# A grouped-query decode block on one core: SyncE keeps the first six loads, GpSimd issues the other 68

## The chip, the core and the metric

The kernel runs on one core of a Trainium2 chip. A core has a matrix engine (TensorE, PE), three engines for elementwise work (VectorE or DVE, ScalarE or ACT, GpSimd or POOL) and an engine for synchronisation and transfers (SyncE, SP). Each runs its own list of instructions in order, and they wait for each other on semaphores. Data comes from the device's memory through 16 DMA engines; SP, ACT and POOL can each issue a transfer, and the DMA engines then carry it out. The metric is the device time of one execution in microseconds (us).

## The reference

Two sequences (B = 2), one token each, are taken through an attention block with a cached history and a gated multilayer perceptron. All is float32.

```
xn = layernorm(x)                                  # x: 2 x 1 x 512
q  = xn @ wq                                       # 32 query heads of 128, 8 key/value heads
s  = softmax(q @ k_cache^T * 128**-0.5) @ v_cache  # 4 query heads share a K/V head
s  = s.reshape(2, 1, 4096) @ wo                    # back to 512
g  = silu((relu(xn @ W_gate) * (xn @ W_up)) @ W_down)   # inner width 1792
out = x + s * g
```

The caches are 2 x 8 x 32768 x 128 each: 268 MB of K and as much of V. All of it is read once, and very little is computed with each byte.

## The kernel before

**Tiles.** For each of the 16 pairs of sequence and K/V head (a group) the 32768 cached tokens are cut into four tiles of 8192 tokens. K and V are loaded two tiles at a time, 8 MB to a load: 128 rows (one for each partition of the on-chip memory) of 64 KB. So there are 32 K loads and 32 V loads; `load_kk(j)` (line 427) and `load_vv(j)` (line 446) issue them for pair j.

**Buffers.** There are three buffers of this size. `kbuf[0]` and `kbuf[1]` take the K pairs in turn, and `wide` takes V. Before that, `wide` holds the query weights wq, then the gate and up weights, then the down weights W_down; at the end, `kbuf[0]` takes one V pair and `kbuf[1]` the output weights wo. A load can be issued when the work that read the buffer's last content is over.

**The loop.** Step j (line 908) does four things: VectorE transposes the K pair j in place in eight pieces (line 679) and TensorE forms its scores (`scores`, line 681); TensorE multiplies the V pair j - 2 by its weights (`values`, line 758); VectorE takes the scores out of the accumulators (line 697); and weights for the next V pair are prepared (lines 748 to 756). A group takes two steps. In odd steps a group's scores are complete: the maximum is found (lines 710 to 738), ScalarE takes the exponentials, and the group whose values are complete is finished: sums (line 775), scaling (line 784), then `finish_group` (line 803), which turns the heads and lets GpSimd copy them into place (line 831). Also in odd steps GpSimd forms the next group's query (`take_query`, lines 544 to 548), when the scores that read the old one are over.

**What sets the order.** Nothing is planned at run time. The program is written as one list of operations (class `Program`, line 31). Each names what it reads and writes, and from that come the waits on other engines; on its own engine each operation keeps its place in the list. So a load waits for its buffer, but it also waits for everything that stands before it on the engine that issues it. Around the change the list of step j reads, shortened:

```
scores(s), [t == 2: mlp_down()], scores(s + 1)   # PE
[odd j: take_query]                              # POOL
values(v), values(v + 1)                         # PE
[odd j: maximum, sums, take_o, finish_group]     # DVE, PE, and POOL at line 831
weights for the next V pair
[j == 0: load_d()  else: load_vv(j - 1)]         # SP
[load_kk(j + 2)]                                 # SP
```

Ahead of the loop SP is given wq, K pair 0, gate, up and K pair 1; in step 0 W_down (`load_d`, line 620) and K pair 2; in step 1 V pair 0 and K pair 3; and so on. After the last step `load_wo` (line 458) issues wo in six pieces. SP has nothing else to do. ScalarE issues two loads of x (4 KB each) and the output.

**Names in the profile.** The K buffers appear as k, `wide` as w, the scores as s, the value sums as o, the down projection as d, the query as qcur. The loads issued by SP have line 248, all matmuls line 251.

Of the kernel before, what the change touches and what calls it, by code (L numbers as in the profile page):

```python
# [167 lines left out]
def decode_block_kernel(nc, x, kc, vc, wq, wo, wg, wu, wd, out):  # L168
# [17 lines left out]
    def sbuf(name, *shape, align=32):  # L186
        return nc.alloc_sbuf_tensor(name, list(shape), F32, align_bytes=align)[:]
# [4 lines left out]
    kbuf = [sbuf(f"k{i}", P, 2 * NC * NR * DH, align=ALIGN) for i in range(2)]  # L192
    wide = sbuf("w", P, 2 * NC * NR * DH, align=ALIGN)
# [53 lines left out]
    def load(dst, src, sem, r=(), w=(), engine="SP"):  # L247
        pg.op(engine, lambda e: e.dma_start(dst, src), r, w, dma=sem)  # L248
# [12 lines left out]
    def group(g):  # L261
        return g % B, g // B
# [50 lines left out]
    for kb in range(4):  # L313
        dve(
            lambda e, kb=kb: e.memset(block_of[Q * kb : Q * kb + Q, kb * REP : (kb + 1) * REP], 1.0),
            w=["block_of"],
# [92 lines left out]
                lambda e, k=k: e.transpose(  # L409
                    px[:, k * 32 : (k + 1) * 32], xquad[:, k, :], ident[:32, :32]  # L410
                )
# [12 lines left out]
    def k_keys(b):  # L424
        return [f"k{b}"] + [f"k{b}_{i}_{c}" for i in range(2) for c in range(NC)]

    def load_kk(j):
        b = j % 2
        load(kbuf[b], rows_of(kc, 2 * j), f"k{b}", w=k_keys(b))

    def rows_of(src, t):
        b, hk = group(t // NU)
        lo = (t % NU) // 2 * 2 * TK
        return src[b, hk, lo : lo + 2 * TK, :].rearrange("(p r) d -> p (r d)", p=P)
# [10 lines left out]

    def load_vv(j):
        if 2 * j == NK - 4:
            load(kbuf[0], rows_of(vc, 2 * j), "k0", w=k_keys(0))
        else:
            load(wide, rows_of(vc, 2 * j), "v", w=["wide"])  # L450

    def in_halves(tokens):
        return tokens.rearrange("p (h c r d) -> p h c r d", h=2, c=NC, d=DH)
# [3 lines left out]
    def load_wo():  # L457
        for quad, cuts in enumerate(((0, 32), (0, 16, 24, 28, 31, 32))):
            dst = kbuf[1][:, quad * ROWS * D : (quad + 1) * ROWS * D]
            WO.append(dst.rearrange("p (j d) -> p j d", j=ROWS))  # L460
            n = ROWS * P
            rows = wo[quad * n : (quad + 1) * n, :].rearrange("(p j) d -> p (j d)", j=ROWS)
            for lo, hi in zip(cuts, cuts[1:]):
                name = f"wo{quad}_{lo}"
                for i in range(lo, hi):
                    WOK[quad, i // 2, i % 2] = name
                load(
                    dst[:, lo * D // 2 : hi * D // 2],
                    rows[:, lo * D // 2 : hi * D // 2],
                    name,  # L470
                    w=[*k_keys(1), name] if quad == 0 else [name],
                )

    def project_q():
# [396 lines left out]
    def project_far():  # L871
# [29 lines left out]
        )  # L901

    load_kk(0)
    project_q()
    load_gu()
    load_kk(1)

    for j in range(PAIRS + 2):
        s, v = 2 * j, 2 * (j - 2)
# [40 lines left out]
        if j == 0:  # L950
            load_d()
        elif j < PAIRS - 1:
            load_vv(j - 1)
        if j == PAIRS - 2:
            load_vv(PAIRS - 2)
        if j + 2 < PAIRS:
            load_kk(j + 2)
        if j == PAIRS - 1:
            load_vv(PAIRS - 1)
            load_wo()  # L960
# [68 lines left out]
```

## Time and profile before

| | us |
|---|---|
| median of three runs | 1309.55 (1309.3 to 1309.71) |
| span of the profiled execution | 1308.7 |
| median less span | 0.85 |
| TensorE busy | 854.4 (65%) |
| VectorE busy | 715.9 (55%) |
| ScalarE busy | 51.3 (4%) |
| GpSimd busy | 12.1 (1%) |
| bytes moved by DMA | 564.81 MB, mean 432 GB/s |

A profile records one execution: when each instruction began, how long it took, and what released the engine that had been idle before it. The rows that are quoted from it have these forms. An instruction in order of time gives its start, its length (both in us), engine, line, operation, what it writes and reads, and in brackets how long its engine had been idle and what ended that. Equal instructions that follow each other are one row with their count; its length reaches from the first to the last. "SPq" and "ACTq" are a queue's own issuing of a transfer. A row of the DMA issues gives the line's tensor, the count, the size, and the time from the issue until the data has landed. A row by stretches gives the stretch, its length, the busy time and the count of instructions of PE, of PE's weight loads, of DVE, ACT and POOL, then the granted clock of TensorE, the busy share of the 16 DMA engines and the GB/s. The row "DMA" with 40 digits is the busy share of the DMA engines, in tenths, in 40 equal slices of the span. "q1" is the queue that SP's loads go through, with its packets, megabytes and share.

### The profile page before, as it was taken

What the parts mean: (1) busy time and instruction counts of PE and PEld (TensorE: products, weight loads), DVE (VectorE), ACT (ScalarE), POOL (GpSimd) and SP (SyncE); (2) the same over time, 40 slices, a digit from 0 to 9 for tenths busy, and PEclk for the clock granted to TensorE, in tenths of its full rate; (3) what the DMA queues carried; (4) which work ended last, traced back from release to release, by engine and by line L of the source; (5) the groups of instructions that cost most, each with busy time, mean ns of one, the idle gap of its engine ahead of it and who ended that gap; (6) DMA issues with size and microseconds to landing.
All of it is one profiled execution on the core that took longest, in us unless ns stands there. A gap on an engine that the chain in (4) does not pass through costs nothing.

```text
span 1308.7 us, 11351 instructions
## 1 busy us (share of the span) xinstructions
PE 854.4 (65%) x4824; PEld 214.3 (16%) x4824; DVE 715.9 (55%) x682; ACT 51.3 (4%) x133; POOL 12.1 (1%) x43
## 2 busy tenths in 40 slices
PE   3566675775566577566667756566765767766685
PEld 1111121211112121111111111111111212111122
DVE  2566554565645466664546665455565545656521
ACT  0001000000000000000000000000000000000000
POOL 0000000000000000000000000000000000000000
PEclk9678788987878888887898788789778788878888
DMA  9999999999999999999999999999999999999998
GB/s 417 425 439 429 441 425 439 425 443 429 437 429 441 427 439 427 439 435 435 441 429 439 427 441 427 439 427 439 445 427 439 429 439 429 439 427 439 435 433 362
DMA packets 10710, 564.81 MB, mean 432 GB/s; under 512 B 1226, under 2 KB 1354, under 8 KB 1612
## 3 DMA queue, kind: packets, MB, share of 16 engines
q1 hardware_dynamic: 10656, 564.66, 99.7%
q8 instruction: 7, 0.11, 0.0%
q14 instruction: 3, 0.02, 0.0%
q10 hardware_dynamic: 44, 0.01, 0.0%
HBM read 564.67 MB, written 0.00 MB: 431 GB/s over the span
## 4 chain that ended last, share of the span: by engine, by line
DMA 64%; DVE 18%; PE 14%; issue 4%; SPq 0%
DMA k<-in_A_k_cache_dram 59%; DVE k L679 18%; PE o L251 8%; PE s L251 5%; DMA k<-in_A_wo_dram 4%; DMA w<-in_A_wq_dram 2%; PE m_ps L251 1%; PE m_ps L712 0%; SPq L248 0%; DVE gy L896 0%; DVE gy L898 0%
## 5 line engine op out<-in xcount | busy, mean ns | idle before, releaser
L251 PE MATMUL s<-k,qcur 128*32 128x512 f32 x2048 | 496.1, 691 | 374.5 <-DVE k L679 374.2
L679 DVE STREAM_TRANSPOSE k<-k 128x2048 f32<-128x2048 f32 x256 | 565.2, 2275 | 146.8 <-DMA k<-in_A_k_cache_dram 146.8
L251 PE MATMUL o<-w,wt 128*16 128x512 f32 x1984 | 245.1, 596 | 10.3 <-DMA w<-in_A_v_cache_dram 10.3
L251 PEld LDWEIGHTS s<-k,qcur 128*32 128x32 f32 x2048 | 88.2, 121 | 782.9 <-DVE k L679 644.4
L756 DVE STREAM_TRANSPOSE wt<-pt 128x512 f32<-128x512 f32 x64 | 45.9, 717 | 140.4 <-PE pt L251 136.1
L697 DVE TENSOR_SCALAR_CACHE_REDUCE st<-s 128x512 f32<-128x512 f32 x64 | 43.0, 672 | 117.4 <-PE s L251 117.4
L251 PEld LDWEIGHTS o<-w,wt 128*16 128x16 f32 x1984 | 62.4, 97 | 168.5 <-issue 168.5
L741 ACT ACTIVATE st<-st,nb 128x512 f32<-128x512 f32 x64 | 45.4, 710 | 1109.5 <-DVE nb L738 1109.5
L251 PE MATMUL pt<-st,perm 128*128 128x512 f32 x128 | 76.0, 725 | 1.5 <-ACT st L741 1.5
L782 DVE RECIPROCAL rl<-m_ps 128x1 f32<-128x1 f32 x16 | 2.7, 168 | 112.0 <-PE m_ps L251 112.0
L251 PE MATMUL m_ps<-ob,heads 128*128 128x128 f32 x128 | 23.6, 341 | 29.0 <-DVE ob L796 29.0
L251 PEld LDWEIGHTS pt<-st,perm 128*128 128x128 f32 x128 | 26.6, 230 | 35.5 <-issue 31.7
L822 DVE STREAM_TRANSPOSE os<-m_ps 128x512 f32<-128x512 f32 x16 | 11.5, 717 | 25.5 <-PE m_ps L251 25.5
L251 PEld LDWEIGHTS m_ps<-ob,heads 128*128 128x128 f32 x128 | 19.7, 235 | 31.1 <-DVE ob L796 31.1
L251 PE MATMUL m_ps<-w,wt 128*32 128x512 f32 (+1 forms) x128 | 16.1, 633 | 8.1 <-DMA w<-in_A_wq_dram 8.1
L796 DVE SCALAR_TENSOR_TENSOR ob<-o,share,ob 128x128 f32<-128x128 f32 x48 | 16.8, 351 | 1.7
L548 POOL TENSOR_TENSOR qcur<-qall,block_of 128x128 f32<-128x128 f32 x16 | 6.5, 407 | 1007.4 <-PE s L251 974.6
L251 PE MATMUL m_ps<-negone,mrow 1*128 1x1 f32 x32 | 6.0, 256 | 9.3 <-DVE mrow L727 9.3
L741 ACT ACTIVATION_READ_ACCUMULATOR st<-st,nb 128x1 f32 x64 | 11.9, 186 | 0.0
L499 DVE COPY os<-m_ps 128x512 f32<-128x512 f32 x2 | 1.4, 690 | 16.1 <-PE m_ps L251 16.1
L409 PE MATMUL m_ps<-ident,st 32*128 32x32 f32 x4 | 0.7, 307 | 14.3 <-DVE st L398 14.3
L251 PE MATMUL s<-k,ots 128*32 128x64 f32 (+1 forms) x176 | 8.1, 324 | 1.5 <-DMA k<-in_A_wo_dram 0.9
(81 smaller groups left out, 102.2 us busy)
## 6 DMA issues: line engine op xcount, KB each, us to landing
k<-in_A_wo_dram SPq DMA_DIRECT2D x1, 4096.0 KB, 39.0
w<-in_B_W_gate_dram SPq DMA_DIRECT2D x1, 3584.0 KB, 19.5
w<-in_B_W_up_dram SPq DMA_DIRECT2D x1, 3584.0 KB, 27.6
w<-in_B_W_down_dram SPq DMA_DIRECT2D x1, 3584.0 KB, 16.1
k<-in_A_wo_dram SPq DMA_DIRECT2D x1, 2048.0 KB, 43.4
k<-in_A_wo_dram SPq DMA_DIRECT2D x1, 1024.0 KB, 45.4
k<-in_A_k_cache_dram SPq DMA_DIRECT2D x32, 48.4
k<-in_A_wo_dram SPq DMA_DIRECT2D x1, 512.0 KB, 46.2
```

The costliest lines, as they stand in the source:

```text
L251: return lambda e: e.matmul(out_, lhs, rhs, start=start, stop=stop, skip_group_check=True)
L409: lambda e, k=k: e.transpose(px[:, k * 32 : (k + 1) * 32], xquad[:, k, :], ident[:32, :32])
L499: dve(lambda e, q=qs, h=half: e.tensor_copy(q, pq[h]), [f"m{half}"], [f"os{half}"])
L548: lambda e: e.tensor_tensor(qcur.rearrange("p e (k h) -> p e k h", h=REP), qall[:, b, hk].unsqueeze(2).to_broadcast([P, 4, Q // REP, REP]) ...
L679: dve(lambda e: e.transpose(at_, at_), [f"k{t // 2 % 2}"], [key])
L697: lambda e: e.tensor_scalar(st[u], ps_s[t % 2], SCALE, None, op0=ALU.mult, op1=ALU.max, accum_out=mx[:, u : u + 1],),
L741: lambda e, u=u: e.activation(st[u], st[u], AF.Exp, bias=nb, scale=1.0, accum_out=ls[:, u : u + 1]),
L756: dve(lambda e: e.transpose(wt[t % 2], ps_p[t % 2]), [f"pt{t % 2}"], [f"wt{t % 2}"])
L782: dve(lambda e: e.reciprocal(rl, ps_m[1][:, :1]), ["m1"], ["rl"])
L796: lambda e, part=part, c=c: e.scalar_tensor_tensor(ob, part, share[:, c : c + 1], ob, op0=ALU.mult, op1=ALU.add),
L822: lambda e: e.transpose(ot, ps_m[1].rearrange("p (h q j) -> p j h q", h=REP, j=ROWS)),
```

## The change

`load` (line 247) issues from SP unless it is told an engine. The change names GpSimd for the K loads from pair 2 on, for all V loads and for the six pieces of wo. On SP remain wq, K pairs 0 and 1, the gate, up and down weights. The two early K loads get semaphores of their own names (h0, h1), and the later ones keep k0 and k1. Buffers, sizes, the list of operations and its order are the same.

```diff
     def load_kk(j):
         b = j % 2
-        load(kbuf[b], rows_of(kc, 2 * j), f"k{b}", w=k_keys(b))
+        early = j < 2
+        load(kbuf[b], rows_of(kc, 2 * j), f"h{b}" if early else f"k{b}", w=k_keys(b), engine="SP" if early else "POOL")
...
     def load_vv(j):
         if 2 * j == NK - 4:
-            load(kbuf[0], rows_of(vc, 2 * j), "k0", w=k_keys(0))
+            load(kbuf[0], rows_of(vc, 2 * j), "k0", w=k_keys(0), engine="POOL")
         else:
-            load(wide, rows_of(vc, 2 * j), "v", w=["wide"])
+            load(wide, rows_of(vc, 2 * j), "v", w=["wide"], engine="POOL")
...
                     rows[:, lo * D // 2 : hi * D // 2],
                     name,
                     w=[*k_keys(1), name] if quad == 0 else [name],
+                    engine="POOL",
                 )
```

## The prediction

> **What bounds the kernel now.** First I read the page's head, the slices and the queues, then the busy time by stretch, to see whether anything but the transfers sets the time.
>
> ```profile
> span 1308.7 us, 11351 instructions
> DMA  9999999999999999999999999999999999999998
> q1 hardware_dynamic: 10656, 564.66, 99.7%
> 150.00:1250.00 1100.00, 732.57 (x3951) 177.03 (x3954) 628.88 (x570) 40.99 (x112) 8.57 (x28) 0.83 1.00 434
> ```
>
> The last row is the stretch from 150 to 1250 us: TensorE 733 us, VectorE 629, DMA share 1.00 at 434 GB/s. The stream is the bound, and no engine is. A K or V load is 8.389 MB (128 rows of 64 KB), so 8.389 MB / 434 GB/s = **19.33 us**. All 564.66 MB at that rate are 1301.1 us, so only 7.6 us of the span lie outside the stream. The time can hardly fall below 1301; and a microsecond in which the DMA engines have nothing to do is lost for good. The question is whether the change ever lets the queue run dry.
>
> Then I read when loads are issued (SP's own rows) and when the loaded K tiles are first used (VectorE's rows), because the distance between them is the slack.
>
> ```profile
> 0.74 0.38 SPq L248 DMA_DIRECT2D w<-in_A_wq_dram  x1
> 32.93 0.44 SPq L248 DMA_DIRECT2D k<-in_A_k_cache_dram  x1
> 72.36 0.33 SPq L248 DMA_DIRECT2D w<-in_B_W_down_dram  x1
> 72.73 0.49 SPq L248 DMA_DIRECT2D k<-in_A_k_cache_dram  x1
> 95.25 0.33 SPq L248 DMA_DIRECT2D w<-in_A_v_cache_dram  x1
> 101.42 0.33 SPq L248 DMA_DIRECT2D k<-in_A_k_cache_dram  x1
> 138.17 0.33 SPq L248 DMA_DIRECT2D w<-in_A_v_cache_dram  x1
> 174.63 0.33 SPq L248 DMA_DIRECT2D w<-in_A_v_cache_dram  x1
> ...
> 80.05 17.66 DVE L679 STREAM_TRANSPOSE k<-k 128x2048 f32<-128x2048 f32 x8 [4.88 <-DMA k<-in_A_k_cache_dram]
> 146.39 17.66 DVE L679 STREAM_TRANSPOSE k<-k 128x2048 f32<-128x2048 f32 x8 [5.59 <-DMA k<-in_A_k_cache_dram]
> 185.00 17.66 DVE L679 STREAM_TRANSPOSE k<-k 128x2048 f32<-128x2048 f32 x8 [0.95 <-DMA k<-in_A_k_cache_dram]
> ...
> w<-in_B_W_down_dram SPq DMA_DIRECT2D x1, 3584.0 KB, 16.1
> w<-in_A_wq_dram SPq DMA_DIRECT2D x1, 22.1
> ```
>
> VectorE takes K pair 3 when it lands at 146.39 and pair 4 at 185.00, two transfers of 19.33 us apart. Counting back from 146.39 over V pair 0 and K pair 3, K pair 2 had landed at 107.7. W_down landed at 72.36 + 16.1 = 88.5, before it, since it was issued first in one queue. V pair 0, issued at 95.25, was 12.4 us ahead of the moment the queue would have been empty (107.7); the V load issued at 138.17 was 8.2 us ahead of 146.39, the one at 174.63 10.4 us ahead of 185.00.
>
> **The change, part by part.** Bytes, buffers and waits on data are the same; of SP's 74 issues (0.3 to 0.5 us each, beside a full stream) 68 move to GpSimd; W_down is the sixth that stays. What matters is order: the loads are now queued behind GpSimd's own work, and no longer behind SP's W_down.
>
> *(1) The hand-over.* K pair 2 waits only for the scores of tiles 0 and 1. On SP it stood behind W_down, which waits for the gate and up matmuls.
>
> ```profile
> 65.73 0.59 PE L251 MATMUL s<-k,qcur 128*32 128x512 f32 x1
> 66.06 6.28 PE L251 MATMUL m_ps<-w,wt 128*32 128x448 f32 x58
> 1.42 1.20 ACTq L248 DMA_DIRECT2D st<-in_A_x_dram  x1
> 10.39 0.67 DVE L382 TENSOR_REDUCE stat<-st 32x1 f32<-32x512 f32 x1 [5.71 <-DMA st<-in_A_x_dram]
> ```
>
> Those scores end at 66.32, so GpSimd issues K pair 2 at 66.4, 6 us before W_down (72.36), while K pair 1 is still arriving (landed 80.05). Is a load on another engine's queue served beside SP's? The rows of x say yes: issued by ScalarE at 1.42 while wq (landed 0.74 + 22.1 = 22.85) and a K load stood ahead on SP's queue, it was in use at 10.39. So K pair 2 shares the DMA engines with K pair 1 and then with W_down. The total of bytes is unchanged: all three are in by 107.7, as before. But W_down, last issued, with 28 KB rows against 64 KB ones, now lands at the end of that stretch, near 107.7 instead of 88.5. K pair 1 lands somewhere between 80 and 91 (11 us of it are left when K pair 2 starts at about 68 and at worst run at half rate).
>
> What hangs on W_down: TensorE's order is scores 2, down projection, scores 3. GpSimd's order is the query multiply for group 1 (line 548, waits for scores 3), then V pair 0, then K pair 3. Before, V pair 0 needed only the down projection.
>
> ```profile
> 91.59 0.61 PE L251 MATMUL d<-w,wt 128*32 128x512 f32 x3
> 92.02 3.17 PE L251 MATMUL d<-w,wt 128*32 128x512 f32 x25
> 118.88 3.63 PE L251 MATMUL s<-k,qcur 128*32 128x512 f32 x28 [1.15 <-DVE k L679]
> 101.47 0.41 POOL L548 TENSOR_TENSOR qcur<-qall,block_of 128x128 f32<-128x128 f32 x1 [65.19 <-PE s L251]
> ```
>
> The down projection takes 91.59 to 95.19 = 3.6 us. Scores 3, whose transposes are done by then (91 + 17.66 = 108.7), take 32 matmuls at 3.63/28 = 4.15 us. The query multiply follows within 0.05 us and takes 0.41. V pair 0 is issued at 107.7 + 3.6 + 4.15 + 0.46 = 115.9.
>
> The price of an issue: on SP wq took 22.1 us to land on an idle chip, less 19.33 leaves **2.8 us** of start and completion. GpSimd's is not in the trace. From below, nothing more than SP's (or 0.4 less, its whole 0.38 row); from above, x's 8.97 us from issue to use, 6.2 more, but that load came in beside a running stream. In between stands ScalarE's issue row, 1.20 against 0.38. I take that, as the other compute engine that issues: +0.8, so 3.6. V pair 0 lands at 115.9 + 3.6 + 19.33 = 138.8; before, 107.7 + 19.33 = 127.0. **The stream stands still: +11.8 us** (11.0 without the 0.8).
>
> The Trainium skill's page "DMA: Bandwidth & Descriptors" (section Latency and other measured facts) gives a first byte after about 1 us on GpSimd's software path against 0.6 on the hardware path. By it the term would be an estimated 11.4, not 11.8. No row here shows it.
>
> After that K pair 3 follows V directly, lands at 158.2, and the step of pair 2 has its V issued at about 152.5 (all its work 12 us later but for 2 us of waiting that it no longer has), 5.7 us ahead. The loss is kept, not repeated.
>
> *(2) The steady steps.* Even steps have no GpSimd work; 8 to 10 us of slack cover 3.6. In each odd step the loads now stand behind the head copy of line 831, at the end of the chain sums, maximum, o, transpose.
>
> ```profile
> 174.95 0.17 DVE L782 RECIPROCAL rl<-m_ps 128x1 f32<-128x1 f32 x1 [6.23 <-PE m_ps L251]
> 179.93 0.72 DVE L822 STREAM_TRANSPOSE os<-m_ps 128x512 f32<-128x512 f32 x1 [2.17 <-PE m_ps L251]
> 180.71 0.20 POOL L831 COPY ots<-os 32x16 f32<-32x16 f32 x1 [12.49 <-DVE os L822]
> 258.98 0.20 POOL L831 COPY ots<-os 32x16 f32<-32x16 f32 x1 [11.56 <-DVE os L822]
> 262.67 17.66 DVE L679 STREAM_TRANSPOSE k<-k 128x2048 f32<-128x2048 f32 x8 [2.03 <-DMA k<-in_A_k_cache_dram]
> 1109.12 0.21 POOL L831 COPY ots<-os 32x16 f32<-32x16 f32 x1 [11.56 <-DVE os L822]
> 1112.69 2.31 DVE L679 STREAM_TRANSPOSE k<-k 128x2048 f32<-128x2048 f32 x1 [1.92 <-DMA k<-in_A_k_cache_dram]
> ```
>
> V moves from 174.63 to 180.91, 4.1 us before the K ahead of it lands (185.00) instead of 10.4. The distances in the other groups lie between 3.4 (1109.33 to 1112.69) and 5.1; 3.5 at 259.18 to 262.67. Against 3.6 only some four of 15 fall short, by 0.1 to 0.2: **+0.4 us in all**. If the cover were thinner by 1.2 us (an issue of 4.8), ten or so would fall short by 0.2 to 1.4, together some 10 us.
>
> *(3) The end.* Six output-weight issues (2.81 us on SP) come behind V pair 31, whose 19.33 us hide them at three times that price. Nothing waits behind them on GpSimd but the last head copy, 37 us later. SP's freed time is worth nothing. **0 us.**
>
> Sum: 11.8 + 0.4 + 0 = 12.2. The profiled execution would have a span of 1308.7 + 12.2 = 1320.9; the median lies 0.85 above the span (1309.55), so **1321.7 us**.
>
> **Rivals.** *(a) Not slower: SP's queue keeps precedence.* If the engines finish what SP has queued before they take GpSimd's, K pair 1 lands at 80.05 and W_down at 88.5 as now, scores 3 end as now, and V pair 0 is issued behind the query multiply at 101.9; 3.6 later is 105.5, before 107.7. No gap, and with (2)'s 0.4: **1310.0**. It decides from a landing of W_down by 107.7 - 3.6 - 0.46 - 4.15 - 3.6 = 95.9, and of K pair 1 by 82.3 (21.3 us from landing to the end of scores 3). For it: x took 9 us for 4 KB, so the newcomer was not served at once. Against it: it did not wait for wq.
>
> *(b) K pair 2 goes as a block.* If its 64 KB rows are taken in one turn once K pair 1 is interrupted, K pair 1 lands 19.33 later, at 99.4, scores 3 end at 120.7, V lands at 121.2 + 3.6 + 19.33 = 144.1: a gap of 17.1, **1327.0**. The rows of x do not tell turns of one row from turns of eight. The Trainium skill, "DMA: Bandwidth & Descriptors" (Queues, rings and completion order), has each engine go round between queues by packets of typically 9 to 17 descriptors; by it this load's eight rows per engine would be one turn, which is this rival.
>
> *(c) The issue is dearer.* At 5.4 us instead of 3.6, the hand-over costs 13.6 and the odd steps' shortfalls (5.4 less 3.4 to 5.1) some 17: **1340**.
>
> *(d) The stream runs slower.* GpSimd's loads might be cut into shorter pieces.
>
> ```profile
> 1257.18 2.81 SPq L248 DMA_DIRECT2D k<-in_A_wo_dram  x6
> k<-in_A_wo_dram SPq DMA_DIRECT2D x1, 4096.0 KB, 39.0
> k<-in_A_wo_dram SPq DMA_DIRECT2D x1, 2048.0 KB, 43.4
> ```
>
> The 2 MB piece with 16 KB rows landed 43.4 + 0.47 - 39.0 = 4.9 us after the one before it: 430 GB/s, 1% less. On 62 loads that is some 11 us more, **1333**. At a DMA share of 1.00 the 434 GB/s leave no room that this trace shows for a gain.
>
> *(e) The change does not do what it says:* GpSimd's loads join SP's queue. Then K pair 2, issued first, goes ahead of W_down, which again lands at 107.7; without the 0.8, 1320.5. It is counted with the forecast.
>
> **How the numbers follow.** Forecast (with e) 0.50; (a) 0.20; (b) 0.10; (c) 0.13; (d) 0.07. A measurement of this kernel tells about 0.2%, 2.6 us, from no change. Of (a) I give 0.15 to within that and 0.05 to faster, since only 7.6 us lie outside the stream; all others are slower: 0.80. The range reaches from just under (a), 1309, to (c) with a little, 1341; what is left out is dearer issues, most of (d)'s shorter cuts, and faster.
>
> **What would show it.** Right: GpSimd issues K pair 2 near 66.4, W_down lands after 100, V pair 0 is issued near 116 and the transposes of K pair 3 start near 158, with DMA below 9 in the slices around 110 and full after. Wrong by (a): W_down lands before 96 and K pair 3 at 146. (b): the transposes of K pair 1 start near 99. (c): the distance between K landings in odd and even steps grows over 38.7 us. (d): the stretch 150 to 1250 shows under 432 GB/s with a share of 1.00.

## The result and the profile after

The changed kernel took 1334.05 us (median of five, 1328.21 to 1337.69) against 1309.47: a ratio of 1.0186 with a 95% interval of 1.0175 to 1.0198. It is slower by 24.6 us, where 12.2 were forecast. The five times of the kernel before lie within 0.4 us, those after it within 9.5.

The profiled execution has a span of 1335.2, 26.5 over the one before. First the head of the page after, the queues, and the busy time by stretch (columns as before: stretch, length, PE, weight loads, DVE, ACT, POOL, granted clock, DMA share, GB/s).

```profile
span 1335.2 us, 11351 instructions
DMA  9995999999999999999999999999999999999998
q0 software_dynamic: 9632, 528.49, 92.0%
q1 hardware_dynamic: 864, 36.18, 6.3%
...
150.00:1250.00 1100.00, 721.33 (x3936) 175.64 (x3928) 615.71 (x564) 40.99 (x112) 39.30 (x86) 0.83 1.00 430
...
107.60:114.00 6.40, 6.35 (x36) 1.62 (x40) 2.27 (x3) 0.00 (x0) 0.00 (x0) 0.56 0.00 0
114.00:118.00 4.00, 3.45 (x32) 0.76 (x21) 0.39 (x1) 0.00 (x0) 0.33 (x1) 1.00 0.00 0
```

GpSimd's loads have a queue of their own (q0) with 528 of the 565 MB. One slice of the span, the one around 110 us, has fallen from 9 to 5; from 107.6 to 118.0 nothing at all is moved. And the long stretch from 150 to 1250 runs at 430 GB/s, no longer 434, with the busy share still at 1.00.

The hand-over, in order of time:

```profile
65.13 0.71 POOL L248 DMA_DIRECT2D k<-in_A_k_cache_dram  x1 [27.84 <-PE s L251]
70.87 0.33 SPq L248 DMA_DIRECT2D w<-in_B_W_down_dram  x1
91.61 17.66 DVE L681 STREAM_TRANSPOSE k<-k 128x2048 f32<-128x2048 f32 x8 [17.95 <-DMA k<-in_A_k_cache_dram]
107.65 5.94 PE L251 MATMUL d<-w,wt 128*32 128x512 f32 x26 [3.47 <-DMA w<-in_B_W_down_dram]
113.42 0.60 PE L251 MATMUL d<-w,wt 128*32 128x512 f32 x2
113.42 4.02 PE L251 MATMUL s<-k,qcur 128*32 128x512 f32 x30
117.67 0.40 POOL L550 TENSOR_TENSOR qcur<-qall,block_of 128x128 f32<-128x128 f32 x1 [51.83 <-PE s L251]
118.02 0.59 POOL L248 DMA_DIRECT2D w<-in_A_v_cache_dram  x1
160.64 17.66 DVE L681 STREAM_TRANSPOSE k<-k 128x2048 f32<-128x2048 f32 x8 [1.80 <-DMA k<-in_A_k_cache_dram]
...
w<-in_B_W_down_dram SPq DMA_DIRECT2D x1, 3584.0 KB, 36.7
```

K pair 2 is issued ahead of W_down; K pair 1 lands at 91.6 instead of 80.05; W_down lands at 70.87 + 36.7 = 107.6 instead of 88.5; down projection, scores 3 and the query multiply follow one after the other, and only then does V pair 0 go out. K pair 3 is taken up at 160.64, **14.25 us** after its place before (146.39).

An odd step later on (the V issue, then VectorE's start on the K pair that was in front of it, and on the next):

```profile
273.72 0.20 POOL L833 COPY ots<-os 32x16 f32<-32x16 f32 x1 [11.57 <-DVE os L824]
273.86 0.59 POOL L248 DMA_DIRECT2D w<-in_A_v_cache_dram  x1
277.23 17.66 DVE L681 STREAM_TRANSPOSE k<-k 128x2048 f32<-128x2048 f32 x8 [1.86 <-DMA k<-in_A_k_cache_dram]
318.11 2.31 DVE L681 STREAM_TRANSPOSE k<-k 128x2048 f32<-128x2048 f32 x1 [9.59 <-DMA k<-in_A_k_cache_dram]
```

V goes out right behind the head copy, 3.37 us before the K pair ahead of it lands, and the next K pair comes 40.88 us later. Two transfers take 38.65; 2.2 us are lost in this step.

The last K pair and the last V pair show how much of this adds up. The first two rows are of the kernel before, the next two of the one after.

```profile
1228.58 6.70 DVE L679 STREAM_TRANSPOSE k<-k 128x2048 f32<-128x2048 f32 x3 [6.04 <-DMA k<-in_A_k_cache_dram]
1286.67 8.65 PE L251 MATMUL o<-w,wt 128*16 128x512 f32 x64 [10.34 <-DMA w<-in_A_v_cache_dram]
```

```profile
1252.63 4.51 DVE L681 STREAM_TRANSPOSE k<-k 128x2048 f32<-128x2048 f32 x2 [7.78 <-DMA k<-in_A_k_cache_dram]
1312.60 9.77 PE L251 MATMUL o<-w,wt 128*16 128x512 f32 x64 [10.88 <-DMA w<-in_A_v_cache_dram]
```

| stretch | before | after | more |
|---|---|---|---|
| start to K pair 3 | 146.39 | 160.64 | 14.25 |
| K pair 3 to K pair 31 | 1082.19 | 1091.99 | 9.8 |
| K pair 31 to the last V | 58.09 | 59.97 | 1.9 |
| last V to the end | 22.0 | 22.6 | 0.6 |

So the loss sits in two places: 14 us at the hand-over, which was forecast, and some 12 in the later steps, of which 0.4 were forecast.

### The profile page after: what moved, and what is told of

It is laid out like the page before. It is cut to its first block, busy times and chain, and to the rows that moved or that the text cites. A ratio compares the mean times of both kernels' runs of the same rounds, so it can differ in the third digit from the quotient of the medians.

```text
span 1335.2 us, 11351 instructions
## 1 busy us (share of the span) xinstructions
PE 855.9 (64%) x4824; PEld 213.9 (16%) x4824; DVE 715.9 (54%) x682; ACT 51.3 (4%) x133; POOL 48.3 (4%) x111
## 4 chain that ended last, share of the span: by engine, by line
DMA 57%; DVE 21%; PE 16%; issue 4%; POOL 1%; SPq 0%
DMA k<-in_A_k_cache_dram 51%; DVE k L681 18%; PE o L251 8%; PE s L251 5%; DMA k<-in_A_wo_dram 3%; DMA w<-in_B_W_down_dram 3%; PE m_ps L251 3%; DVE ob L798 1%; DVE os L824 1%; POOL w L248 1%; PE d L251 0%; DVE ob L792 0%; DVE share L787 0%; POOL ots L833 0%; DVE mr L719 0%
## 5 line engine op out<-in xcount | busy, mean ns | idle before, releaser
L251 PEld LDWEIGHTS s<-k,qcur 128*32 128x32 f32 x2048 | 88.5, 122 | 803.0 <-DVE k L681 660.9
L251 PE MATMUL pt<-st,perm 128*128 128x512 f32 x128 | 72.3, 693 | 1.3 <-ACT st L743 1.3
L248 POOL DMA_DIRECT2D w<-in_A_v_cache_dram x31 | 17.4, 560 | 488.8 <-PE o L251 487.8
L248 POOL DMA_DIRECT2D k<-in_A_k_cache_dram x30 | 16.1, 537 | 27.8 <-PE s L251 27.8
L833 POOL COPY ots<-os 32x16 f32<-32x16 f32 x16 | 3.3, 206 | 243.9 <-DVE os L824 243.9
## 6 DMA issues: line engine op xcount, KB each, us to landing
w<-in_B_W_down_dram SPq DMA_DIRECT2D x1, 3584.0 KB, 36.7
```

The costliest lines, as they stand in the source:

```text
L251: return lambda e: e.matmul(out_, lhs, rhs, start=start, stop=stop, skip_group_check=True)
L833: lambda e: e.tensor_copy(ots[mine, : 2 * ROWS * 32].rearrange("p (q j m) -> p q j m", q=2, j=ROWS)[:, hk // 4, :, SHIFT + b * APART], ot[ ...
```

## The experiments

Each time below is a median on the chip, set against the kernel before on the same chip (1309.4 to 1309.5). A ratio is the record's estimate over the executions and not the quotient of the two medians; where the executions scatter, the two differ by up to 1.8 us. The changed kernel itself scatters by 9.5 us, so a share of its loss that is taken from two medians holds to within a few us.

### Each of the two places undone alone

**K pair 2 stays on SP.** The edit, to the changed kernel:

```diff
-        early = j < 2
+        early = j < 3
...
-            pg.emit("PE", e, sems, loop=(NU, NK))
+            pg.emit("PE", e, sems, loop=(2 * NU, NK))   # likewise ACT and DVE
```

> SyncE keeps seven loads: K pair 2 stays on SP behind the down weights; everything else as in the changed kernel (the loop of the engines starts one round later, so that K pair 2 can have a semaphore of its own). Theory (two places: the hand-over, and the odd steps whose loads stand behind the head copy): the hand-over's 14.2 us go, 1334.1 - 14.2 = 1320, K pair 3 starts near 146.4, and the losses in the later steps stay. Rival (GpSimd's stream is slower on every load, about 0.2 us on each of 61): also 1320, but the distance between K landings grows by the same 0.3 to 0.4 us in all steps. Rival (the 24 us come from the later steps alone, the hand-over is caught up): stays above 1330.

Measured: 1318.94 us (1316.93 to 1321.26), a ratio of 1.0079 (1.0062 to 1.0096). That is 15.1 under the changed kernel. The hand-over is worth what the trace shows there; some 9.5 us remain.

**The loads listed ahead of the head copy.** In the changed kernel, the block that issues a step's loads is moved up:

```diff
             mlp_fold()
+        [if j == 0: load_d() ... load_vv, load_kk, load_wo as below]
         if ends:
             if live:
                 tile_maximum()
...
-        [the same block]
```

> The changed kernel with each step's loads listed right after the values, so that on GpSimd they stand ahead of the head copy and no longer behind it. Theory: the odd steps get back their 10 us of cover, the distances between K landings fall to 38.65 in both kinds of step, and the time falls by some 10 to 12 us to 1322 to 1324; the hand-over's 14 us stay. Rival (the stream itself is slower): no change, 1334.

Measured: 1323.44 us (1322.77 to 1323.84), ratio 1.0106 (1.0089 to 1.0122): 10.6 under the changed kernel. In odd steps V now goes out 8.4 to 10.2 us ahead, as before the change, and the distances between K landings are 38.6 to 38.7 from pair 5 on. The odd steps cost 10.6, and it is the place in GpSimd's list that costs it.

**Both.**

> Both of the above undone: K pair 2 on SP, and GpSimd's loads ahead of the head copy. Theory: nothing of the loss is left, 1309.5 to 1312, with the stretch 150 to 1250 at 434 GB/s through GpSimd's queue. Rival (slower stream): 1320.

Measured: 1309.61 us (ten executions, 1309.41 to 1309.93), ratio 1.0002 (0.9992 to 1.0012). The stretch from 150 to 1250 in its trace:

```profile
150.00:1250.00 1100.00, 738.49 (x3943) 178.12 (x3946) 629.00 (x569) 40.99 (x112) 38.81 (x84) 0.83 1.00 434
```

434 GB/s again, through GpSimd's queue. 67 loads issued by GpSimd cost nothing as long as they keep their order and their lead. With both undone, all of the 24.6 us is gone; taken alone the two are 15.1 and 10.6, together within 1.1 of the whole.

### The hand-over without the rest

**K pair 2 alone on GpSimd**, all else on SP (with the same later start of the loop):

```diff
-        load(kbuf[b], rows_of(kc, 2 * j), f"k{b}", w=k_keys(b))
+        load(kbuf[b], rows_of(kc, 2 * j), "g0" if j == 2 else f"k{b}", w=k_keys(b), engine="POOL" if j == 2 else "SP")
```

> The kernel before with K pair 2 alone on GpSimd; V pair 0 and all later loads stay on SP. Theory: W_down still lands last, near 107.6, the down projection ends near 113.5, and V pair 0 (on SP it does not stand behind the query multiply) is issued there, 4.5 us before its place in the changed kernel (118.0): the loss is 14 - 4.5 = 9 to 10, 1318 to 1320, and the later steps lose nothing. Rival (the loss comes with GpSimd's stream as a whole, not with this one load): 1309.5.

Measured: 1321.62 us (1321.02 to 1323.03), ratio 1.0095 (1.0079 to 1.0112): one load on another queue costs 12.1 us. V pair 0 went out at 112.92, as soon as the down projection was over, some 5 us before its place in the changed kernel, and K pair 3 was taken up at 156.17, 9.8 us later than in the kernel before, as expected. The whole time came out some 2 us over the expectation; the next three steps of the trace lose 0.9 of them, and the rest was not found.

**K pair 2 alone on ScalarE**, with `engine="ACT"` in that line (and the early pairs' semaphores named h0 and h1).

> As the run before, but K pair 2 is issued by ScalarE, whose queue is of SP's kind. Theory (any second queue that takes K pair 2 past W_down and shares the DMA engines does it): as with GpSimd, 1318 to 1320. Rival (it is GpSimd's way of issuing): 1309.5 to 1312.

Measured: 1322.52 us (1319.12 to 1324.01), ratio 1.0091 (1.0074 to 1.0108). That is again over the 1318 to 1320 that were expected, with executions 5 us apart. The traces of the two (first GpSimd's, then ScalarE's) read alike:

```profile
65.00 0.72 POOL L248 DMA_DIRECT2D k<-in_A_k_cache_dram  x1 [29.43 <-PE s L251]
89.37 17.66 DVE L679 STREAM_TRANSPOSE k<-k 128x2048 f32<-128x2048 f32 x8 [15.84 <-DMA k<-in_A_k_cache_dram]
```

```profile
64.67 0.35 ACTq L248 DMA_DIRECT2D k<-in_A_k_cache_dram  x1
91.42 17.66 DVE L679 STREAM_TRANSPOSE k<-k 128x2048 f32<-128x2048 f32 x8 [17.95 <-DMA k<-in_A_k_cache_dram]
```

The hand-over is not about GpSimd. A second queue of either kind takes the load past W_down.

**All 74 loads on GpSimd**, in the list's order and ahead of the head copy: one queue, nothing to pass.

> All 74 loads on GpSimd, in the list's order, each step's loads listed right after the values and so ahead of the head copy. One queue, so K pair 2 stands behind W_down again. Theory: no loss at the hand-over and none in odd steps, 1309.5 to 1311.5. wq, issued on an idle chip, tells the price of one issue: 22.1 us to landing on SP; 22.9 if GpSimd costs 0.8 more, 22.1 or less if it costs nothing more.

Measured: 1310.31 us (nine executions from 1310.08 to 1310.48), ratio 1.0006 (0.9996 to 1.0016). A tenth execution took 1889.45 us; it has no trace, and nothing on record says why. wq, issued on an idle chip, landed after this time:

```profile
w<-in_A_wq_dram POOLq DMA_DIRECT2D x1, 22.3
```

On SP it was 22.1 in the kernel before and 21.8 in the changed one. By this load GpSimd's issue costs 0.2 to 0.5 us more, not 0.8. The traces also list every packet (in a load of wq, K or V one row of 64 KB, moved by one DMA engine): wq's first packet began 1.03 us after the issue on SP (kernel before) and 1.39 us after it on GpSimd (this run).

### Why the odd steps lose

The forecast had 3.4 to 5.1 us of lead against a price of 3.6. If GpSimd's price is no larger than that, why are 10 us lost?

**SP as late as GpSimd.** The kernel before, with one wait added:

```diff
-            load(wide, rows_of(vc, 2 * j), "v", w=["wide"])
+            load(wide, rows_of(vc, 2 * j), "v", r=behind, w=["wide"])   # behind: the head copy's key, in odd steps
```

> The kernel before, all loads on SP, with one wait added: in odd steps the V load also waits for the head copy on GpSimd, so it is issued as late as in the changed kernel, but through SP's queue. Theory as predicted (cover of 3.4 to 5.1 against a price of an issue of 2.8 on SP): no loss, 1309.5 to 1311. Rival (the cover is too thin for any queue, since single DMA engines run empty before the slowest one has landed): up to 10 us more, 1319.

Measured: 1322.77 us (1320.24 to 1324.02), ratio 1.0096 (1.0079 to 1.0113). The expectation fell: SP loses 13 us in the same place. One of its steps:

```profile
336.77 0.20 POOL L831 COPY ots<-os 32x16 f32<-32x16 f32 x1 [12.48 <-DVE os L822]
337.00 0.33 SPq L248 DMA_DIRECT2D w<-in_A_v_cache_dram  x1
341.18 17.66 DVE L679 STREAM_TRANSPOSE k<-k 128x2048 f32<-128x2048 f32 x8 [2.32 <-DMA k<-in_A_k_cache_dram]
381.32 4.50 DVE L679 STREAM_TRANSPOSE k<-k 128x2048 f32<-128x2048 f32 x2 [6.74 <-DMA k<-in_A_k_cache_dram]
```

With a lead of 4.18 the next K pair comes after 40.14 us: 1.5 lost, though wq's price on an idle chip had been read as 2.8.

**Later still, on SP and on GpSimd.** To measure the two prices where both must show, V waits in odd steps until the second tile's weights have been turned. `after` adds a wait on what last wrote a key, and nothing else:

```diff
-        for k in reads:
+        for k in (*reads, *after):
             if k in self.wrote:
                 need(self.wrote[k])
...
-            load_vv(j - 1)
+            load_vv(j - 1, ["wt1"] if ends and summed else ())
```

> The kernel before, all loads on SP, but in odd steps the V load also waits until VectorE has turned the second tile's weights, about 1 us before the K load ahead lands. Such a lead is under any price, so the loss is 15 times the needed lead less about 1. If SP needs 4.5 (what the kernel with the wait for the head copy suggests): 15 x 3.5 = 52, 1362. If SP needs 2.8 (my reading of the first load): 15 x 1.8 = 27, 1336.

> The same wait, but with the loads from V pair 0 on issued by GpSimd (K pair 2 stays on SP, so there is no loss at the hand-over). Its time less the one through SP, divided by 15, is what an issue on GpSimd costs more. As predicted (0.8 us): 12 us above it. Rival (no dearer, the queue makes no difference): within 3 us of it.

Measured: 1330.48 us (1327.68 to 1332.88) through SP, ratio 1.0153 (1.0136 to 1.0170), and 1331.99 us (1330.58 to 1336.72) through GpSimd, ratio 1.0184 (1.0165 to 1.0202). The medians differ by 1.5 us, the ratios by 4, and the executions of either by 5 to 6, so the rival (within 3) is nearer than the 12 that were predicted. A price in each step cannot be read from the difference, since the leads are not the same: 1.6 to 2.0 in 13 steps through GpSimd, 0.9 to 2.0 in ten steps and 3.5 to 3.6 in four through SP. The packets tell it. To engines that stood idle, SP's first packet came 0.95 to 1.0 us after the issue, and GpSimd's 1.3 to 1.4 (1.29 for V pair 0 of the changed kernel). So GpSimd's issue is some 0.3 to 0.4 us dearer, which is too little to see in these times. And the loss through SP is 21, short of both numbers that were expected. A lead shorter by 3 us costs only some 8 us more than the head copy's. A step through SP, and one through GpSimd:

```profile
421.12 0.33 SPq L248 DMA_DIRECT2D w<-in_A_v_cache_dram  x1
422.09 17.66 DVE L679 STREAM_TRANSPOSE k<-k 128x2048 f32<-128x2048 f32 x8 [1.00 <-DMA k<-in_A_k_cache_dram]
462.25 4.51 DVE L679 STREAM_TRANSPOSE k<-k 128x2048 f32<-128x2048 f32 x2 [9.28 <-DMA k<-in_A_k_cache_dram]
```

```profile
890.79 0.59 POOL L248 DMA_DIRECT2D w<-in_A_v_cache_dram  x1 [3.03 <-DVE wt L758]
892.37 17.66 DVE L681 STREAM_TRANSPOSE k<-k 128x2048 f32<-128x2048 f32 x8 [1.88 <-DMA k<-in_A_k_cache_dram]
932.28 4.50 DVE L681 STREAM_TRANSPOSE k<-k 128x2048 f32<-128x2048 f32 x2 [7.57 <-DMA k<-in_A_k_cache_dram]
```

With a lead of 1.0 us SP loses 40.16 - 38.64 = 1.5, about as much as with 4.18.

**Shorter pieces at the end of each K load.** SP behind the head copy once more, and K loads cut in two:

```diff
-        load(kbuf[b], rows_of(kc, 2 * j), f"k{b}", w=k_keys(b))
+        def emit(e):   # cut: three quarters of a partition's 64 KB
+            e.dma_start(kbuf[b][:, :cut], src[:, :cut]).then_inc(sems[f"k{b}"], 16)
+            return e.dma_start(kbuf[b][:, cut:], src[:, cut:])
```

> All loads on SP, V in odd steps behind the head copy as in the run with that wait (1322.8), and each K load cut in two, with its last quarter in rows of 16 KB instead of 64 KB, so that the last pieces of a draining load take 0.6 us of a DMA engine instead of 2.4. Theory (an engine needs its next piece while the last long one is still under way): the needed lead falls by up to 1.8 us, below the 3.4 to 5.1 there is, and the time falls to 1310 to 1313. Rival (the lead is needed for the issue itself, whatever drains): stays at 1321 to 1324.

> The kernel before with its K loads cut the same way and no wait added: what the cutting costs by itself. Theory: nothing, 1309 to 1311, since the stream never runs empty. Rival: 16 KB rows are 1% slower, a quarter of the K bytes, 1.5 us more.

Measured: 1316.03 us (1314.50 to 1321.70), ratio 1.0064 (1.0039 to 1.0088); the cutting alone 1310.75 us, ratio 1.0010 (1.0001 to 1.0020). By the medians the added wait costs 13.4 us with long last pieces and 5.3 with short ones; by the ratios, 12.6 and 7. So it fell, by how much is uncertain, and neither expectation came true: three executions lie over the theory's 1310 to 1313 and under the rival's 1321 to 1324, and one, at 1321.70, within the rival's. A step with a lead of 3.63 in which next to nothing is lost (38.89):

```profile
956.76 0.33 SPq L248 DMA_DIRECT2D w<-in_A_v_cache_dram  x1
960.39 17.66 DVE L685 STREAM_TRANSPOSE k<-k 128x2048 f32<-128x2048 f32 x8 [0.94 <-DMA k<-in_A_k_cache_dram]
999.28 2.31 DVE L685 STREAM_TRANSPOSE k<-k 128x2048 f32<-128x2048 f32 x1 [8.02 <-DMA k<-in_A_k_cache_dram]
```

**The loss by lead.** For each step of each trace: the lead is VectorE's start on a K pair less the V issue before it; the loss is the distance to the next start less 38.64. The mean loss in us, with the count of steps in brackets:

| kernel | under 2.2 | 3.0 to 3.65 | 3.65 to 4.35 | 4.35 to 5.6 | over 8 |
|---|---|---|---|---|---|
| before (SP) | | | | | 0.0 (28) |
| changed (GpSimd) | | 1.1 (4) | 0.6 (6) | 0.1 (5) | 0.1 (12) |
| K pair 2 on SP, rest GpSimd | | 1.1 (3) | 0.2 (3) | 0.1 (8) | 0.2 (13) |
| SP behind the head copy | | 0.9 (4) | 1.0 (7) | 0.0 (3) | 0.1 (13) |
| SP later still | 1.8 (10) | 0.7 (4) | | | 0.1 (13) |
| GpSimd later still | 1.2 (13) | 2.3 (1) | | | 0.1 (14) |
| SP behind the copy, short pieces | | 0.7 (4) | 0.1 (2) | 0.1 (8) | 0.1 (13) |

A lead over some 4.4 us costs next to nothing, with 64 KB rows: of 16 such steps under 5.6 (three on SP, 13 on GpSimd) one lost 1.0. From 3.0 to 4.35 a step loses 0.9 on average, and from 0.9 to 2.2 no more than 1.2 (through GpSimd) to 1.8 (through SP). Within a column steps scatter by up to 2 us, and some with a lead of 3.5 lose nothing. With 16 KB rows at the end of the load ahead, four steps with leads of 3.63 to 4.16 lose 0.05 to 0.25, which suggests a lower edge. But that trace also has more steps over 4.35, eight of 14 against three of 14 in the run with the wait alone, so it does not show how much of the gain is the edge and how much the longer leads.

**What the packets show.** In the kernel before, a 64 KB packet takes an engine 2.42 us, and between 150 and 1250 us an engine has nothing to do for 0.1 us. In the changed kernel an engine has nothing to do for 2.9 us there, and 169 packets take over 2.6 us, up to 3.9, against five before; that makes 7.1 us more for each engine. Together with 2.8 us more of idle time that is 9.9, next to the 9.8 lost between K pair 3 and K pair 31. In the run later still on SP the two are 9.2 and 12.0, together near the 21 that were lost. So most of the changed kernel's second loss is not idle time: around a late issue, packets take longer. In the SP step shown above, V was issued at 421.12, the engines finished K between 420.78 and 421.77, V's packets began from 422.09 on, and these first 16 took 2.8 to 3.4 us. wq's first 16, on the idle chip, took 3.04 on average. A shorter lead adds idle time and hardly changes this part, so the loss grows little. Why such packets take longer, no run shows.

The packets also say what a lead has to cover. Each packet begins where another has ended, and so they can be strung together into 16 engines. A K pair has landed when the last engine is done, and VectorE starts 0.3 to 0.4 us after that. In the kernel before the engines finish a K load 1.9 to 2.1 us apart, in the run later still on SP 0.4 to 2.9. With the 1.0 from issue to first packet, an estimate of the needed lead on SP is some 3.3 us for engines 1.9 apart, and 4.3 for engines 2.9 apart. In that run a step with a lead of 3.53 and engines 2.1 apart lost 1.7, and three with 3.57 to 3.58 and engines 0.5 to 0.7 apart lost 0.1 to 0.6. So the 4.4 is no fixed price: it depends on how far apart the engines are.

## Why the prediction was right, and where it was not

The measured 1334.05 lies within the stated range of 1309 to 1341 and 12.4 above the forecast of 1321.7. The part of the loss that was forecast is the hand-over; the range holds the rest only because it reaches up to rival (c), and neither (c) nor (d) is what happened. That (d)'s 1333 lies next to the measured time is luck.

**The hand-over (term 1, +11.8).** Right in its mechanism at every link, each now seen in the rows above: GpSimd issued K pair 2 at 65.1 (66.4 forecast), W_down landed at 107.6 (107.7), V pair 0 left at 118.0 (115.9), and DMA stood still in between. Single runs confirm that this order makes the loss: K pair 2 back on SP gives back 15.1, K pair 2 alone on GpSimd takes 12.1, on ScalarE 13. The size was 2.4 short in the trace. 2.1 of it is V pair 0's later issue: the down projection took 107.65 to 114.02, 6.4 us, where 3.6 had been read from the kernel before, and the query multiply then came 3.65 behind it instead of 4.2. The other 0.4 lie behind the issue: K pair 3 was taken up 42.62 after it, 3.96 over two transfers, where 3.6 was forecast. The windows give the reason for the longer down projection: after its wait TensorE was granted a mean clock of 0.56 there. This row of the kernel before shows 1.00 for the same work, and 3.70 us at 1.00 are 6.6 at 0.56:

```profile
91.50:95.20 3.70, 3.70 (x36) 1.13 (x30) 3.70 (x2) 0.00 (x0) 0.00 (x0) 1.00 0.74 319
```

A duration taken from one place of a trace was moved to another where the clock was lower.

One reading in this part does not follow from its words: V pair 1 at 138.17, 12 us later but for 2, is 148 and not 152.5. It was issued at 156.47, 4.17 us ahead of K pair 3 and not 5.7, and that step lost 0.35.

**The price of an issue (0.8 more on GpSimd).** Wrong, without much harm. On an idle chip it is 0.2 to 0.5 by the landing, and 0.3 to 0.4 by the first packet, in the loop as well. ScalarE's 1.20 us row was no measure for GpSimd's, whose own rows are 0.53 to 0.71. The page "DMA: Bandwidth & Descriptors" of the Trainium skill (Latency and other measured facts) has 0.4 between the two ways; these figures agree.

**The steady steps (term 2, +0.4).** This is the step that failed. Putting the loads behind the head copy costs 10.6 us, not 0.4. That the loads would stand there, and about the lead that would be left (3.4 to 5.1 forecast, 3.2 to 5.4 in the trace), were right. Wrong was the sentence that weighed this lead against "a price" of 3.6, and with it the rule that a step loses price less lead. The price had been read from a load that met an idle chip. In the stream the lead counts to the landing of the last engine, while the first ones are done up to 2.9 us earlier; some 4.4 was needed on SP as well, and SP lost 13 us with GpSimd's leads, so the loss does not come from GpSimd's queue. And a step that falls short loses more than the shortfall, since its packets take longer; why they do stays open. The prediction had itself worked out that a need of 4.8 would cost some 10 us, next to the measured 10.6, and left that out of its sum.

**The end (0).** Right to within a microsecond: 0.6 behind the last V. The last odd step lost 1.9 like the others.

**The rivals.** (a) SP's queue keeps precedence: no, W_down landed at 107.6. (b) K pair 2 goes as a block: no, K pair 1 landed at 91.6 (89.4 and 91.4 in the single runs), at the forecast's bound of half rate (91), not at 99. By the packets, while K pair 1 and K pair 2 were both under way, each engine of the changed kernel took one 64 KB row of either queue in turn. A turn of eight rows, which the prediction worked out from the packet of nine to 17 descriptors that the Trainium skill names ("DMA: Bandwidth & Descriptors", Queues, rings and completion order), is not how these two queues took turns. (c) Dearer issues: its sign, distances over 38.7, came in odd steps, but GpSimd's price is not the reason. (d) A slower stream: its sign, under 432 GB/s at a share of 1.00, came too, but with order and lead restored GpSimd's queue ran at 434. The signs of both could not tell them from a lead that is too short; the runs did. (e) One common queue: no, q0 stands beside q1.

**A sentence on reading.** The prediction took a DMA share of 1.00 as the sign that nothing is lost. After the change the share is still 1.00 at 430 GB/s. The rate told of the loss and the share did not, since packets that take longer count as busy.

## What to carry to other kernels

Moving transfers to another engine moves them past two lists: out of the order with what stays on the old queue, where a large late load can overtake a small one that the next work waits for, and in behind the new engine's own instructions. Hand over at a point where nothing urgent is left on the old queue, and list the loads ahead of work that is not theirs; then the issuing engine made no difference here (1309.6 against 1309.4). Where DMA is the bound, ask of every issue how far ahead of the stream's end it comes, and measure the lead that is needed in the running stream, not from the first load.

## What the runs showed that was not expected

- A load of 64 KB rows had to be issued some 4.4 us before the load ahead of it had landed to be safe, on SP as on GpSimd; below that a step lost 0.9 us on average, and with a lead of one to two us no more than 1.2 to 1.8.
- Of the 9.9 us that the changed kernel loses between 150 and 1250 us, 7.1 are packets that take longer (up to 3.9 us instead of 2.42) and 2.8 are idle engines.
- Cutting the last quarter of each K load into 16 KB rows took the cost of the late issue from 13.4 to 5.3 us by the medians (12.6 to 7 by the ratios), and cost 1.3 by itself.
- The kernels that lose time scatter by 1 to 9.5 us between executions, the others by 0.6 or less, but for the one execution of 1889.45.
- Waiting 3.5 us for W_down, TensorE came back at a mean clock of 0.56 for 6.4 us, and was at 1.00 right after.
